# A causal-attention and gated-MLP kernel: fp32r weighted sums issued in one piece, residuals planned behind both copies, and a third matrix group in the weighted sums' bank

## The chip, the cores and the metric

The kernel runs on one core of a Trainium2 chip. The metric is device time in microseconds (us) of one execution, and the median of several. TensorE multiplies 128x128 weights with a stream of columns and adds into banks of PSUM. VectorE (DVE), ScalarE (ACT) and GpSimd (POOL) copy and compute, SyncE (SP) issues the transfers. Each engine works through its own instructions in order and waits on semaphores for the others.

## The reference

```python
scores = scale * np.matmul(q, k.transpose(0, 1, 3, 2))      # q, k, v: (4, 12, 448, 64)
scores = np.where(mask, -1000000000.0, scores)              # causal
attn = np.exp(scores - max); attn = attn / (sum + 1e-09)
attn_out = np.matmul(attn, v)
x = attn_out.transpose(0, 2, 1, 3).reshape(1792, 768)
g = x @ w_gate                                              # (768, 1536)
return ((g / (1 + exp(-g))) * (x @ w_val)) @ w_out          # w_out: (1536, 768)
```

## The kernel before

A chunk is one batch: 448 tokens. There are four, and each has attention for six pairs of heads and then the MLP. The MLP takes 24 matrix groups M0 to M23 of 18 products (gate and value in turn, one bank each) and six output tiles MO0 to MO5 of 36. Every product is a 128x448 fp32r matmul; each tile of weights is used three times (high by high, high by low, low by high part) for the precision, so a chunk has 648 products and the kernel 2592. In what follows a "product" is one of these matmuls (lines 850 to 852).

Attention of chunk 0 runs with plain fp32 matmuls. From chunk 1 on, each pair of heads has: fp32r scores (24 matmuls, line 501), softmax on DVE, ACT and POOL, transposes of the probabilities into a bank T (line 680; line 650 for T_0, which both heads share), a copy of T to `ph` (ACT or DVE, lines 309, 312), a residual T minus `ph` to `pl` or to the other half of `ph` (DVE, line 331), and the weighted sum of the values into the bank O (lines 715 and 717). The weighted sum of a head has seven matmuls: 448 columns for block 0, then twice 384, twice 256 and twice 128. After it ACT copies one half of O to `tmp` and DVE adds the other half into `xs`, which frees O.

PSUM has one bank T (chunk 0 also uses the X banks for transposes), one bank O, two banks M for the matrix groups and two each for S and X. A matrix group needs a bank M for itself until DVE has taken its result out (line 886 for a gate, 892 for a value).

The order of everything is made ahead of the run by `Planner.run`. Each operation `op` has a due time, dependencies, buffers (`Res`) and a modelled length for each engine that can do it; the planner always places the operation that can begin first, the earlier due first, and what it makes is the fixed order of every engine. `TURN` adds time for a change between kinds of TensorE work ("m" product or weighted sum, "s" scores, "t" transposes, "v" fp32 sums), `LAT` is the delay from one engine to another. In `weigh`, each of a head's blocks is an operation of its own with a loop variable `last`; in `spread`, the residual `lo` depends only on its own copy `hi`.

Of the kernel before, what the change touches and what calls it, by code (L numbers as in the profile page):

```python
# [17 lines left out]
P = 128  # L18
D = 64
# [19 lines left out]
SHARED = 0.5  # L39
PVLATE = 0  # L40
LAT = {"PE": 0.29, "DVE": 0.2, "ACT": 0.23, "POOL": 0.2, "SP": 0.1}
TURN = {'ms': 0.19, 'sm': 0.19, 'mt': 0.0, 'tm': 0.0, 'ts': 0.19, 'st': 0.19, 'mv': 0.15, 'vm': 0.15, 'tv': 0.15, 'vt': 0.15, 'sv': 0.15, 'vs': 0.15}
TS = 0.0
PF = 1.12
GF = 1.25
# [1 line left out]
SG = [[[0, 3]], [[1, 2]]]  # L47
TV = 0.0
WINDOW = 96
WARM = 22  # L50
FIRST = [[[0, 1]], [[2]], [[3]]]
KBUS = 1 / 320
# [169 lines left out]
def raw(t):  # L222
    return t.bitcast(F32)
# [3 lines left out]
def kernel(  # L227
# [68 lines left out]
    def op(alts, due, deps=(), alloc=(), uses=(), extra=0.0):  # L296
        first = [heads[r.tag] for r in alloc if r.tag in heads]
        o = pl_.op(alts, due, list(deps) + first, alloc, uses, extra)
        o.soft = first
        o.port = bool(alts.pop("port", False))  # L300
        o.kb = alts.pop("kb", 0)
        o.kind = alts.pop("kind", "m")
        for r in alloc:
            heads[r.tag] = o
        return o
# [83 lines left out]
    def attention(u):  # L389
        U = units[u]  # L390
        c, b, h, N, KB = U.c, U.b, U.h, U.n, U.qb
        s = st[u]
# [220 lines left out]
        def spread(g, js, tr, rT, lo_row, kn, n, cols, offs, v2):  # L613

            stk = kn == D
            rh = Res(f"ph{g}")
            src = lambda: s[f"T{g}"][lo_row : lo_row + kn, :n]

            def newh():
                s[f"ph{g}"] = buf([P, n], F32R, f"ph{g}", "ph", f"ph{u}_{g}")  # L620
                return s[f"ph{g}"][lo_row : lo_row + kn]
            hi = op(copies("psum", n, newh, src, engines="AD"), due(8), [tr], [rh], [rT])
            rl = None if stk else Res(f"pl{g}")

            def newl():
                if stk:
                    return s[f"ph{g}"][D - lo_row : P - lo_row]
                s[f"pl{g}"] = buf([P, n], F32R, f"pl{g}", "pl", f"pl{u}_{g}")
                return s[f"pl{g}"][:kn]
            lo = op(binary(n, newl, src, lambda: raw(s[f"ph{g}"])[lo_row : lo_row + kn], engines="D"),  # L630
                    due(9), [hi], [] if stk else [rl], [rT, rh])
            for j, o_, w in zip(js, offs, cols):
                blocks[j] = (g, o_, w, slice(0, P), stk, [hi, lo, v2], [rh, rV] + ([] if stk else [rl]))

        if h % 2:

            rT = Res(ttag(c))
            both_ = [norms[i] for i in norms] + [normed[u - 1][i] for i in normed[u - 1]]

            def transp0(rT=rT):  # L640
                pt = s["T0"] = st[u - 1]["T0"] = bank(rT.tag, f"T{u}_0")
                for i, (q0, _) in U.qi:
                    r = U.rows[i]
                    w = U.qi[i][1][1]
                    if U.joint and i == 0:

                        o = pt.rearrange("p (a b) -> p a b", b=D)[:, :: N // D]
                        nc.tensor.transpose(o, s["pp0"], ident)
                        continue
                    nc.tensor.transpose(pt[:, q0 : q0 + r], s[f"pp{i}"][:r, w - D : w + D], ident[:r, :r])  # L650
            tr = op({"PE": (0.109 * len(U.qi), transp0), "kind": "t"}, due(7), both_, [rT], list(rps.values()) + ([prps[u - 1][0]] if U.joint else []))
            if npv:
                rh = Res("ph0")

                def newp():
                    s["ph0"] = st[u - 1]["ph0"] = buf([P, NJ], F32, "ph0", "ph", f"ph{u}_0")
                    return s["ph0"]
                NJ = N + D * U.joint
                hi = op(copies("psum", NJ, newp, lambda: s["T0"][:, :NJ], engines="AD"), due(8), [tr], [rh], [rT])
                for y in (0, 1):  # L660
                    parts[u - 1 + y][0] = (0, 0, N, slice(D * y, D * y + D), True, [hi, lv], [rh, rv])
            else:
                first0[u - 1](tr, rT)
                spread(0, [0], tr, rT, D, D, N, [N], [0], v2)
        elif not npv:
            first0[u] = lambda tr, rT: spread(0, [0], tr, rT, 0, D, N, [N], [0], v2)

        for g, js in enumerate([[1], [2, 3]], 1):
            cols = [U.qb - U.base(j) for j in js]
            offs = [sum(cols[:i]) for i in range(len(js))]  # L670
            n = sum(cols)
            rT = Res(ttag(c))
            todo = [(j, o_, i, e) for j, o_ in zip(js, offs) for i, e in U.qi if e[0] >= U.kb[j][0]]

            def transp(g=g, todo=todo, rT=rT):
                pt = s[f"T{g}"] = bank(rT.tag, f"T{u}_{g}")
                for j, o_, i, (q0, q1_) in todo:
                    r, bs, (k0, k1) = U.rows[i], U.base(j), U.kb[j]
                    k0 = k0 if h % 2 else q1_ - k1
                    nc.tensor.transpose(pt[:, o_ + q0 - bs : o_ + q0 - bs + r], s[f"p{i}"][:r, k0 : k0 + P], ident[:r, :r])  # L680
            tr = op({"PE": (0.109 * len(todo), transp), "kind": "t"}, due(7),
                    [norms[i] for i in {i for _, _, i, _ in todo}], [rT], [rps[i] for i in {i for _, _, i, _ in todo}])
            if npv:
                rh = Res(f"ph{g}")

                def newh(g=g, n=n):
                    s[f"ph{g}"] = buf([P, n], F32, f"ph{g}", "ph", f"ph{u}_{g}")
                    return s[f"ph{g}"]
                hi = op(copies("psum", n, newh, lambda g=g, n=n: s[f"T{g}"][:, :n], engines="AD"), due(8), [tr], [rh], [rT])
                for j, o_, w in zip(js, offs, cols):  # L690
                    blocks[j] = (g, o_, w, slice(0, P), False, [hi, lv], [rh, rv])
            else:
                spread(g, js, tr, rT, 0, P, n, cols, offs, v2)
        if h % 2 and not npv:
            weigh(u - 1)
        if h % 2:
# [2 lines left out]
    def weigh(u):  # L699
# [4 lines left out]
        k = h // 2  # L704
        prevx = [xlast[k]] if k in xlast else []
        if not npv:
            rO, last = Res("O"), None
            for j in range(nj):
                g, o_, w, _, stk, dps, use = blocks[j]

                def pv(g=g, j=j, o_=o_, w=w, stk=stk):
                    if j == 0:
                        s["O"] = bank("O", f"O{u}")
                    O, V = s["O"][:, U.base(j) - U.qa : N], s["VS"][:, j, :]
                    nc.tensor.matmul(O, V, s[f"ph{g}"][:, o_ : o_ + w], start=(j == 0), stop=stk and j == nj - 1)  # L715
                    if not stk:
                        nc.tensor.matmul(O, V, s[f"pl{g}"][:, o_ : o_ + w], start=False, stop=(j == nj - 1))  # L717
                last = op({"PE": ((1 if stk else 2) * cost("PE", "r", w), pv)}, due(10), dps + [last],
                          [rO] if j == 0 else [], use + ([rO] if j else []))
            rx, rt = Res(f"xs{h}"), Res("tmp")  # L720

            def newt():
                s["tmp"] = buf([D, S], F32, "tmp", "tmp", f"tmp{u}")[:, :N]
                return s["tmp"]
            t1 = op(copies("psum", N, newt, lambda: s["O"][D:P, :N], engines="AD"), due(11), [last], [rt], [rO])
            o = op(binary(N, lambda: xs[k][D * (h % 2) : D * (h % 2) + D, :N], lambda: s["O"][0:D, :N],
                          lambda: s["tmp"], ALU.add, engines="D"), due(12), [t1] + prevx, [rx], [rO, rt])
            xs_ops.setdefault((c, k), []).append(o)
            xs_res.setdefault((c, k), []).append(rx)
            return  # L730
# [123 lines left out]
    def moe(c):  # L854
# [6 lines left out]
        for f in range(NF):  # L861
            rt = Res("t")
            tops = {}
            for w in range(2):
                gi = 2 * f + w
                i = base + gi
                wh_, wl_, rwh, rwl = wops[i]
                rM = Res("M")
                prev = None
                for k in range(KD):  # L870
                    xa, xb, rxh, rxl = xsplit[c, k]

                    def mm(k=k, f=f, w=w, i=i, gi=gi):
                        if k == 0:
                            ps[c, f, w] = bank("M", f"M{c}_{gi}")
                        mm3(ps[c, f, w], i, k, N, xh[k][:, :N], xl[k][:, :N], k == 0, k == KD - 1)
                    prev = op({"PE": (m3, mm)}, at(gi + k / KD), [prev, wh_, wl_, xa, xb],
                              [rM] if k == 0 else [], [rwh, rwl, rxh, rxl] + ([rM] if k else []))
# [50 lines left out]
    for c in range(NCHUNK):  # L929
# [2 lines left out]
                attention(u)  # L932
        for k in range(KD):
            split_x(c, k)
    for c in range(NCHUNK):
        moe(c)
    order = pl_.run(CAPS)
    with tc.manual_schedule():
# [53 lines left out]
```

## Time and profile before

| what | value |
|---|---|
| median of 3 runs | 697.47 us (696.21 to 697.72) |
| the profiled execution: its time | 697.56 us |
| the profiled execution: its span, first to last instruction | 695.8 us |
| TensorE busy | 685.6 us, 99% of the span |
| DVE, ACT, POOL busy | 353.4, 335.8, 197.1 us |
| granted TensorE clock | 0.999 of full speed |

The span is what the trace shows; 1.8 us of the execution lie around it. The order of TensorE decides the time wherever it is busy, and the other engines matter where TensorE waits for them.

### The profile page before, as it was taken

Reading aid. Unit: us, or ns where it says so; the run is one execution under the profiler, and the core shown is the slowest. Engines: PE = TensorE matmul, PEld = TensorE weight load, DVE = VectorE, ACT = ScalarE, POOL = GpSimd, SP = SyncE. Lnnn points to the kernel's source line nnn. Section 1 sums busy time; section 2 is a strip of 40 time slices with the busy share of each in tenths; the row PEclk is TensorE's granted clock in tenths of the full one; section 3 lists DMA queues with packets and bytes.
Section 4 is the critical chain, followed back from the end, with each engine's and each line's share of the span. In section 5 each row is a group of like instructions: output and inputs, shape, how many; then the busy total and the mean of one; then the engine's idle time right before and its main releaser. Section 6 shows DMA issues by size and latency. Waiting matters only on the chain.

```text
span 695.8 us, 10844 instructions
## 1 busy us (share of the span) xinstructions
PE 685.6 (99%) x3898; PEld 603.3 (87%) x3898; DVE 353.4 (51%) x880; ACT 335.8 (48%) x835; POOL 197.1 (28%) x250
## 2 busy tenths in 40 slices
PE   8998999999999999999999999999999999999998
PEld 6567898898898988888989889999899999999997
DVE  5878977788875453565542255545544222222100
ACT  6997787688583452543543436445455211111000
POOL 3764446366333332332331213223221000000000
PEclk9999999999999999999999999999999999999999
DMA  8778998998988755655657665554466666666671
GB/s 293 267 274 312 374 330 326 338 354 324 355 333 314 253 183 192 209 167 207 203 196 238 214 202 191 183 182 168 151 200 191 193 221 221 199 216 222 213 239 41
DMA packets 40118, 165.08 MB, mean 237 GB/s; under 512 B 4480, under 2 KB 13952, under 8 KB 40064
## 3 DMA queue, kind: packets, MB, share of 16 engines
q1 hardware_dynamic: 39904, 164.28, 68.6%
q8 instruction: 31, 0.51, 0.3%
q14 instruction: 23, 0.19, 0.1%
q10 hardware_dynamic: 160, 0.10, 0.1%
HBM read 130.55 MB, written 33.82 MB: 236 GB/s over the span
## 4 chain that ended last, share of the span: by engine, by line
PE 84%; DVE 3%; ACT 2%; issue 1%; ACTq 0%; DVEq 0%
PE M L850 15%; PE M L851 15%; PE M L852 15%; PE MO L850 9%; PE MO L851 8%; PE MO L852 8%; PE S L501 4%; PE T L680 3%; PE O L715 3%; PE O L717 2%; PE T L650 1%; DVE ph L331 1%; DVE wraw L833 1%; ACT ph L309 1%; ACT top L309 0%
## 5 line engine op out<-in xcount | busy, mean ns | idle before, releaser
L850 PE MATMUL M<-xh,whl 128*128 128x448 f32 x576 | 216.2, 375 | 1.5 <-DVE t L886 1.5
L851 PE MATMUL M<-xl,whl 128*128 128x448 f32 x576 | 210.3, 365 | 0.4 <-DVE xl L331 0.4
L852 PE MATMUL M<-xh,whl 128*128 128x448 f32 x576 | 209.8, 364 | 0.0
L850 PEld LDWEIGHTS M<-xh,whl 128*128 128x128 f32 x576 | 108.1, 188 | 13.3 <-issue 3.5
L852 PEld LDWEIGHTS M<-xh,whl 128*128 128x128 f32 x576 | 107.9, 187 | 9.1
L851 PEld LDWEIGHTS M<-xl,whl 128*128 128x128 f32 x576 | 108.2, 188 | 8.5 <-DVE xl L331 0.8
L850 PE MATMUL MO<-hh,whl 128*128 128x448 f32 x288 | 107.7, 374 | 0.0
L851 PE MATMUL MO<-hl,whl 128*128 128x448 f32 x288 | 105.1, 365 | 0.0
L852 PE MATMUL MO<-hh,whl 128*128 128x448 f32 x288 | 105.0, 364 | 0.0
L551 ACT ACTIVATE p<-p,m 128x192 f32<-128x192 f32 (+3 forms) x180 | 91.0, 508 | 1.8 <-DVE m L540 1.8
L309 ACT ACTIVATE ph<-T 128x384 fp32r<-128x384 f32 (+3 forms) x104 | 51.9, 507 | 65.4 <-PE T L650 35.5
L540 DVE CUSTOM_DVE_ANT_0 p<-S,masks 128x192 f32<-128x192 f32 (+3 forms) x180 | 67.6, 432 | 25.7 <-PE S L501 25.6
L886 DVE SCALAR_TENSOR_TENSOR t<-t,M 128x448 f32<-128x448 f32 x48 | 29.7, 620 | 60.3 <-ACT t L882 60.1
L309 ACT ACTIVATE hh<-t 128x448 fp32r<-128x448 f32 x39 | 22.5, 576 | 76.4 <-DVE t L892 76.2
L599 POOL TENSOR_SCALAR p<-p,rec 128x192 f32<-128x192 f32 (+3 forms) x66 | 39.9, 613 | 64.5 <-DVE rec L563 45.5
L850 PEld LDWEIGHTS MO<-hh,whl 128*128 128x128 f32 x288 | 54.1, 188 | 4.5 <-issue 0.6
L852 PEld LDWEIGHTS MO<-hh,whl 128*128 128x128 f32 x288 | 54.0, 187 | 4.6
L851 PEld LDWEIGHTS MO<-hl,whl 128*128 128x128 f32 x288 | 54.1, 188 | 3.9
L595 ACT ACTIVATE p<-p,rec 128x192 f32<-128x192 f32 (+3 forms) x114 | 49.9, 488 | 10.7 <-DVE rec L563 10.4
L892 DVE TENSOR_TENSOR t<-t,M 128x448 f32<-128x448 f32 x48 | 29.6, 617 | 48.5 <-PE M L852 48.5
L882 ACT ACTIVATE t<-M 128x448 f32<-128x448 f32 x48 | 26.0, 542 | 57.9 <-PE M L852 57.2
L331 DVE TENSOR_TENSOR pl<-T,ph 128x384 fp32r<-128x384 f32 x72 | 39.7, 551 | 25.6 <-ACT ph L309 25.2
(77 smaller groups left out, 864.4 us busy)
## 6 DMA issues: line engine op xcount, KB each, us to landing
whl<-ws SPq DMA_DIRECT2D x108, 768.0 KB, 4.3
wide<-in_w_dram SPq DMA_DIRECT2D x36, 768.0 KB, 6.9
ws<-whl SPq DMA_DIRECT2D x36, 768.0 KB, 6.7
vraw<-in_v_dram SPq DMA_DIRECT2D x24, 256.0 KB, 4.2
out_dram<-osb SPq DMA_DIRECT2D x24, 224.0 KB, 4.7
qraw<-in_q_dram SPq DMA_DIRECT2D x23, 224.0 KB, 4.2
kraw<-in_k_dram SPq DMA_DIRECT2D x23, 224.0 KB, 4.6
qraw<-in_q_dram SPq DMA_DIRECT2D x1, 128.0 KB, 2.4
```

Of the source, the lines that this page charges most:

```text
L309: nc.scalar.activation(out(), in_(), AF.Copy, scale=scale)
L331: r["DVE"] = (cost("DVE", "two", n), lambda: nc.vector.tensor_tensor(out(), a(), b(), alu))
L501: nc.tensor.matmul(st[u + y][f"S{i}"][: U.rows[i]], Q[:, q0 : q0 + U.rows[i]], K[:, :q1_] if y else K[:, S - q1_ :], start=z == 0, stop=z ...
L540: nc.vector.tensor_tensor_reduce(p[:r], s[f"S{i}"][:r], mask[:r, maskX - q0 : maskX - q0 + q1_] if h % 2 else back[:r, P - min(q1_, P) : P ...
L551: nc.scalar.activation(p[:r], p[:r], AF.Exp, bias=peak(i)[:r], scale=-1.0, accum_out=sums[u % NR][:r, i : i + 1],)
L595: nc.scalar.activation(p[:r], p[:r], AF.Copy, scale=rec[u % NR][:r, i : i + 1])
L599: nc.gpsimd.tensor_scalar(p[:r], p[:r], rec[u % NR][:r, i : i + 1], 0.0, ALU.mult, ALU.add)
L850: nc.tensor.matmul(out[:, :n], a[:, w], xhi, start=first, stop=False)
L851: nc.tensor.matmul(out[:, :n], a[:, w], xlo, start=False, stop=False)
L852: nc.tensor.matmul(out[:, :n], l[:, w], xhi, start=False, stop=last)
L886: nc.vector.scalar_tensor_tensor(t, t, 1.0, ps[c, f, 0][:, :N], ALU.add, ALU.mult)
L892: nc.vector.tensor_tensor(t, t, ps[c, f, 1][:, :N], ALU.mult)
```

## The change

Four edits, all of them to what the planner works with.

- A head's weighted sum becomes one operation of kind "o": its seven matmuls stand together, behind all copies and residuals of that head. `TURN` gets four entries for this kind.
- `spread` returns the copy and a function `rest`. For T_0, which two heads share, both copies are made first, and the even head's residual is planned with a dependency on the odd head's copy as well.
- In chunk 0, matrix group M2 (`SPARE`) takes the bank O in place of a bank M.
- `moe(c)` is called right behind the splitting of `x` of its chunk and no more after all attention, which changes ties between equal due times and the order in which users of a bank are numbered.

```diff
-TURN = {'ms': 0.19, ... 'vs': 0.15}
+TURN = {'ms': 0.19, ... 'vs': 0.15, 'om': 0.055, 'os': 0.1, 'so': 0.19, 'ot': 0.03}
+SPARE = [2]
...
-            lo = op(binary(n, newl, src, lambda: raw(s[f"ph{g}"])[lo_row : lo_row + kn], engines="D"),
-                    due(9), [hi], [] if stk else [rl], [rT, rh])
...
+            def rest(first=()):
+                lo = op(binary(n, newl, src, lambda: raw(s[f"ph{g}"])[lo_row : lo_row + kn], engines="D"),
+                        due(9), [hi, *first], [] if stk else [rl], [rT, rh])
...
-                first0[u - 1](tr, rT)
-                spread(0, [0], tr, rT, D, D, N, [N], [0], v2)
+                (_, even), (hi, odd) = first0[u - 1](tr, rT), spread(0, [0], tr, rT, D, D, N, [N], [0], v2)
+                even([hi])
+                odd()
...
-                last = op({"PE": ((1 if stk else 2) * cost("PE", "r", w), pv)}, due(10), dps + [last],
-                          [rO] if j == 0 else [], use + ([rO] if j else []))
+            last = op({"PE": (dur, pv), "kind": "o"}, due(10), dps, [rO], use)
...
-                rM = Res("M")
+                tag = "O" if c == 0 and gi in SPARE else "M"
+                rM = Res(tag)
...
-    for c in range(NCHUNK):
         moe(c)
```

**Place 1, TensorE, the first products of chunk 0.** `M0_g` is matrix group g of chunk 0, `xh5` and `xl5` the last of the six parts of x. Before:

```order
L850 MATMUL M0_0_746<-xh5_82,whl0_452 128x448 [waits Pool_49]
L851 MATMUL M0_0_746<-xl5_88,whl0_452 128x448 [waits DVE_49]
L852 MATMUL M0_0_746<-xh5_82,whl0_452 128x448
L850 MATMUL M0_1_790<-xh5_82,whl1_607 128x448
L851 MATMUL M0_1_790<-xl5_88,whl1_607 128x448
L852 MATMUL M0_1_790<-xh5_82,whl1_607 128x448
L850 MATMUL M0_2_992<-xh0_77,whl2_773 128x448 [waits DVE_49]
```

Now:

```order
L858 MATMUL M0_2_958<-xh0_77,whl2_773 128x448 [waits Activation_49]
L859 MATMUL M0_2_958<-xl0_83,whl2_773 128x448
L860 MATMUL M0_2_958<-xh0_77,whl2_773 128x448
L858 MATMUL M0_0_746<-xh5_82,whl0_452 128x448 [waits Pool_49]
L859 MATMUL M0_0_746<-xl5_88,whl0_452 128x448 [waits DVE_49]
L860 MATMUL M0_0_746<-xh5_82,whl0_452 128x448
L858 MATMUL M0_1_790<-xh5_82,whl1_607 128x448
L859 MATMUL M0_1_790<-xl5_88,whl1_607 128x448
L860 MATMUL M0_1_790<-xh5_82,whl1_607 128x448
L858 MATMUL M0_2_958<-xh1_78,whl2_773 128x448
```

The first three products of group 2 moved ahead of the last ones of groups 0 and 1, and its first product waits for ACT (who emptied bank O) and no more for DVE (who empties a bank M).

**Place 2, TensorE, the weighted sum of the odd head of the last pair** (head 47, bank `O47`; `MO2_5` is the last output tile of chunk 2, and `ph47_0` to `ph47_2` are the copies of the three transposes). Before, in three pieces, with transposes and nine products between:

```order
L715 MATMUL O47_6174<-ph47_0_6133,VS47_5899 128x448 [waits DVE_49]
L680 MATMUL T47_2_6176<-ident_66,p46_2_5991 128x128 [waits DVE_49,PE_49]
L680 MATMUL T47_2_6176<-ident_66,p46_3_5994 128x128 x2
L715 MATMUL O47_6174<-ph47_1_6163,VS47_5899 128x384
L717 MATMUL O47_6174<-pl47_1_6172,VS47_5899 128x384
...
L852 MATMUL MO2_5_6136<-hh6_95,whl107_6044 128x448
L715 MATMUL O47_6174<-ph47_2_6182,VS47_5899 128x256 [waits Activation_49]
L717 MATMUL O47_6174<-pl47_2_6187,VS47_5899 128x256 [waits DVE_49]
L715 MATMUL O47_6174<-ph47_2_6182,VS47_5899 128x128
L717 MATMUL O47_6174<-pl47_2_6187,VS47_5899 128x128
L850 MATMUL MO2_5_6136<-hh7_96,whl107_6044 128x448
```

Now:

```order
L858 MATMUL MO2_5_6135<-hh7_96,whl107_6046 128x448
L859 MATMUL MO2_5_6135<-hl7_108,whl107_6046 128x448
L860 MATMUL MO2_5_6135<-hh7_96,whl107_6046 128x448
L724 MATMUL O47_6196<-ph47_0_6133,VS47_5902 128x448 [waits Activation_49]
L724 MATMUL O47_6196<-ph47_1_6166,VS47_5902 128x384 [waits Activation_49]
L726 MATMUL O47_6196<-pl47_1_6172,VS47_5902 128x384
L724 MATMUL O47_6196<-ph47_2_6184,VS47_5902 128x256 [waits Activation_49]
L726 MATMUL O47_6196<-pl47_2_6191,VS47_5902 128x256 [waits DVE_49]
L724 MATMUL O47_6196<-ph47_2_6184,VS47_5902 128x128
L726 MATMUL O47_6196<-pl47_2_6191,VS47_5902 128x128
L858 MATMUL MO2_5_6135<-hh8_97,whl107_6046 128x448
```

All seven matmuls stand together, in front of the products of `MO2_5`, and no other piece follows. The even head's seven stood together before as well; three more products now stand between T_0 and them at most pairs.

**Place 3, DVE, the last pair of heads**, from the even head's last residuals. Before:

```order
L331 TENSOR_TENSOR ph46_0_6128<-T47_0_6120,ph46_0_6128 64x448 [waits PE_49,Activation_49]
L331 TENSOR_TENSOR ph47_0_6133<-T47_0_6120,ph47_0_6133 64x448
L312 TENSOR_SCALAR ph47_1_6163<-T47_1_6154 128x384 [waits PE_49]
L331 TENSOR_TENSOR xs5_76<-O46_6145,tmp46_6158 64x448 [waits Activation_49]
L331 TENSOR_TENSOR pl47_1_6172<-T47_1_6154,ph47_1_6163 128x384 [waits DVE_49]
L331 TENSOR_TENSOR pl47_2_6187<-T47_2_6176,ph47_2_6182 128x384 [waits Activation_49]
L331 TENSOR_TENSOR xs5_76<-O47_6174,tmp47_6204 64x448 [waits Activation_49]
```

Now:

```order
L332 TENSOR_TENSOR ph46_0_6128<-T47_0_6120,ph46_0_6128 64x448 [waits PE_49,Activation_49]
L332 TENSOR_TENSOR ph47_0_6133<-T47_0_6120,ph47_0_6133 64x448
L332 TENSOR_TENSOR xs5_76<-O46_6149,tmp46_6161 64x448 [waits Activation_49]
L332 TENSOR_TENSOR pl47_1_6172<-T47_1_6157,ph47_1_6166 128x384 [waits Activation_49]
L332 TENSOR_TENSOR pl47_2_6191<-T47_2_6177,ph47_2_6184 128x384 [waits Activation_49]
L332 TENSOR_TENSOR xs5_76<-O47_6196,tmp47_6207 64x448 [waits Activation_49]
```

The two residuals of T_0 (`ph46_0`, `ph47_0`) stand one behind the other in both programs. The copy of T_1 went from DVE to ACT, so the add into `xs` now comes directly before the residual of T_1.

## Rows read from the trace of the kernel before

**Rows 1.** The page's first part: busy us, share of span, instructions by engine.

```profile
PE 685.6 (99%) x3898; PEld 603.3 (87%) x3898; DVE 353.4 (51%) x880; ACT 335.8 (48%) x835; POOL 197.1 (28%) x250
```

**Rows 2.** The list of waits: us in total, times, longest.

```profile
PEld O L715 <- DVE ph L331: 5.9, 15, 0.7
PE M L850 <- DVE t L886: 1.5, 1, 1.5
```

**Rows 3.** Timeline, TensorE, 58.6 to 63 us: start, length, line, tiles, count [wait].

```profile
58.90 0.36 PE L850 MATMUL M<-xh,whl 128*128 128x448 f32 x1
...
59.64 0.47 PE L851 MATMUL M<-xl,whl 128*128 128x448 f32 x1 [0.39 <-DVE xl L331]
...
60.56 0.36 PE L852 MATMUL M<-xh,whl 128*128 128x448 f32 x1
...
62.38 0.47 PE L850 MATMUL M<-xh,whl 128*128 128x448 f32 x1 [1.47 <-DVE t L886]
```

**Rows 4.** Timeline, DVE, 61 to 63 us.

```profile
61.72 0.61 DVE L886 SCALAR_TENSOR_TENSOR t<-t,M 128x448 f32<-128x448 f32 x1
```

**Rows 5.** Timeline, TensorE, 374 to 378 us: T_0, products, a weighted sum, T_1.

```profile
374.42 0.60 PE L650 MATMUL T<-ident,p 128*128 128x128 f32 x4
...
376.51 0.36 PE L852 MATMUL MO<-hh,whl 128*128 128x448 f32 x1
...
376.85 0.65 PE L715 MATMUL O<-ph,VS 128*128 128x448 f32 x2
...
377.34 0.34 PE L717 MATMUL O<-pl,VS 128*128 128x384 f32 x1
...
377.94 0.52 PE L680 MATMUL T<-ident,p 128*128 128x128 f32 x3
```

**Rows 6.** Timeline, ACT and then DVE, 375 to 379 us.

```profile
375.06 1.09 ACT L309 ACTIVATE ph<-T 64x448 fp32r<-64x448 f32 x2 [2.29 <-PE T L650]
...
378.14 0.54 ACT L309 ACTIVATE tmp<-O 64x448 f32<-64x448 f32 x1 [1.99 <-PE O L717]
...
376.18 1.27 DVE L331 TENSOR_TENSOR ph<-T,ph 64x448 fp32r<-64x448 f32 x2 [5.89 <-ACT ph L309]
...
379.08 0.62 DVE L331 TENSOR_TENSOR xs<-O,tmp 64x448 f32<-64x448 f32 x1
```

**Rows 7.** Timeline, TensorE, 159.5 to 161.3 us: a weighted sum's first three matmuls.

```profile
159.94 0.54 PE L715 MATMUL O<-ph,VS 128*128 128x448 f32 x2
160.32 0.34 PE L717 MATMUL O<-pl,VS 128*128 128x384 f32 x1
```

**Rows 8.** Timeline, TensorE, 133 us: products behind a whole weighted sum.

```profile
132.99 0.42 PE L850 MATMUL M<-xh,whl 128*128 128x448 f32 x1
133.24 0.37 PE L851 MATMUL M<-xl,whl 128*128 128x448 f32 x1
133.45 0.37 PE L852 MATMUL M<-xh,whl 128*128 128x448 f32 x1
```

**Rows 9.** Timeline, TensorE, 367 to 368 us: products, two others between these.

```profile
367.48 0.36 PE L850 MATMUL MO<-hh,whl 128*128 128x448 f32 x1
...
368.08 0.36 PE L850 MATMUL MO<-hh,whl 128*128 128x448 f32 x1
```

**Rows 10.** Timeline, TensorE, from 555 us: behind the last weighted sum, and the last product.

```profile
555.14 0.42 PE L850 MATMUL MO<-hh,whl 128*128 128x448 f32 x1
555.40 0.36 PE L851 MATMUL MO<-hl,whl 128*128 128x448 f32 x1
555.60 0.36 PE L852 MATMUL MO<-hh,whl 128*128 128x448 f32 x1
555.81 0.37 PE L850 MATMUL MO<-hh,whl 128*128 128x448 f32 x1
...
692.00 0.36 PE L852 MATMUL MO<-hh,whl 128*128 128x448 f32 x1
```

More of the change, by code (lines that the diff above doesn't have):

```diff
@@ L41 @@
 LAT = {"PE": 0.29, "DVE": 0.2, "ACT": 0.23, "POOL": 0.2, "SP": 0.1}
-TURN = {'ms': 0.19, 'sm': 0.19, 'mt': 0.0, 'tm': 0.0, 'ts': 0.19, 'st': 0.19, 'mv': 0.15, 'vm': 0.15, 'tv': 0.15, 'vt': 0.15, 'sv': 0.15, 'vs': 0.15}
+TURN = {'ms': 0.19, 'sm': 0.19, 'mt': 0.0, 'tm': 0.0, 'ts': 0.19, 'st': 0.19, 'mv': 0.15, 'vm': 0.15, 'tv': 0.15, 'vt': 0.15, 'sv': 0.15, 'vs': 0.15, 'om': 0.055, 'os': 0.1, 'so': 0.19, 'ot': 0.03}
 TS = 0.0
@@ L629, in newl @@
                 return s[f"pl{g}"][:kn]
-            lo = op(binary(n, newl, src, lambda: raw(s[f"ph{g}"])[lo_row : lo_row + kn], engines="D"),
-                    due(9), [hi], [] if stk else [rl], [rT, rh])
-            for j, o_, w in zip(js, offs, cols):
-                blocks[j] = (g, o_, w, slice(0, P), stk, [hi, lo, v2], [rh, rV] + ([] if stk else [rl]))
+            def rest(first=()):
+                lo = op(binary(n, newl, src, lambda: raw(s[f"ph{g}"])[lo_row : lo_row + kn], engines="D"),
+                        due(9), [hi, *first], [] if stk else [rl], [rT, rh])
+                for j, o_, w in zip(js, offs, cols):
+                    blocks[j] = (g, o_, w, slice(0, P), stk, [hi, lo, v2], [rh, rV] + ([] if stk else [rl]))
+            return hi, rest
         if h % 2:
@@ L692, in attention @@
             else:
-                spread(g, js, tr, rT, 0, P, n, cols, offs, v2)
+                spread(g, js, tr, rT, 0, P, n, cols, offs, v2)[1]()
         if h % 2 and not npv:
@@ L706, in weigh, with pv @@
         if not npv:
[L707 to L713, printed above, removed]
+            rO, dps, use, dur = Res("O"), [], [], 0.0
+            for g, o_, w, _, stk, d_, r_ in (blocks[j] for j in range(nj)):
+                dps += [x for x in d_ if x not in dps]
+                use += [r for r in r_ if r not in use]
+                dur += (1 if stk else 2) * cost("PE", "r", w)
+            def pv():
+                s["O"] = bank("O", f"O{u}")
+                for j in range(nj):
+                    g, o_, w, _, stk, _, _ = blocks[j]
                     O, V = s["O"][:, U.base(j) - U.qa : N], s["VS"][:, j, :]
@@ L871, in moe, with mm @@
                     xa, xb, rxh, rxl = xsplit[c, k]
-                    def mm(k=k, f=f, w=w, i=i, gi=gi):
+                    def mm(k=k, f=f, w=w, i=i, gi=gi, tag=tag):
                         if k == 0:
-                            ps[c, f, w] = bank("M", f"M{c}_{gi}")
+                            ps[c, f, w] = bank(tag, f"M{c}_{gi}")
                         mm3(ps[c, f, w], i, k, N, xh[k][:, :N], xl[k][:, :N], k == 0, k == KD - 1)
```

## The prediction

> **What bounds the kernel now.** I read the page's first part first: TensorE is busy 685.6 of 695.8 us [rows 1], so the time is the sum of what TensorE does, one thing behind the other, and an edit pays only where TensorE's row of starts gets closer. Then the list of waits, and there the entries of TensorE and of its weight loads alone: 5.9 us in 15 waits of a weighted sum's first weight load for DVE's residual, and one of 1.5 us for DVE's gate product [rows 2]. DVE's or ACT's own idle time says nothing here. Then the timeline of TensorE, read by starts, since lengths overlap: what counts is the distance from one start to the next. Three things are to be seen.
>
> First, chunk 0 stalls once. The second product of group 0's last part starts 0.74 us after the first (59.64 against 58.90), and group 2's first product starts 1.82 us after the one ahead of it (62.38 against 60.56) [rows 3]. An undisturbed distance is 0.20 us [rows 9]. The second stall ends when DVE has finished the gate product that began at 61.72 and took 0.61 [rows 4]: group 2 waits for the bank of group 0.
>
> Second, the even head's weighted sum waits at most pairs. The last product ahead starts at 376.51, the sum at 376.85: 0.34 where 0.20 is usual, so 0.14 is lost. The first two matmuls of the sum then take 0.49 (377.34 less 376.85) [rows 5], where a sum that came late enough takes 0.38 [rows 7]: another 0.11. A wait costs 0.25 us. What it waits for [rows 6]: ACT copies T_0 for both heads from 375.06 to 376.15, and only then, at 376.18, DVE starts the two residuals, the first of which ends near 376.81. I count 14 such waits in TensorE's starts from 186.7 to 548.7, two of them longer (0.18 and 0.25 instead of 0.14).
>
> Third, the products have two spacings. Three products take 0.60 us [rows 9], 200 ns each. Behind the last weighted sum they take (692.00 - 555.81) / 659 = 206.7 ns each, to the end [rows 10]. The clock is granted in full all along. A stretch keeps the spacing with which it began until transposes or scores interrupt it. By starts, 1008 of the distances between products are slow ones, 659 in the last stretch. The difference, 6.7 ns, is 4.4 us there and 2.3 us in the 349 others. How a stretch begins shows which it will be: a second distance of 201 to 203 ns leads to 206.7, one of 204 (twice 200) leads to 200. Behind twelve pieces of four matmuls (two of 256 columns, two of 128) the second distance is 0.20 (555.60 less 555.40) and the stretch slow; the last of them is in [rows 10]. Behind a whole sum of seven it is 0.21 (133.45 less 133.24) in the one place that has it, 133 us [rows 8], too short to show the stretch itself.
>
> **The change part by part**, against the profiled 697.56 us (0.09 above the median of 697.47).
>
> *Third group in bank O.* Of the two stalls, 1.62 + 0.54 us beyond the usual 0.20, and 0.1 behind each at the next distance (59.64 to 59.95 is 0.31 instead of 0.20), make 2.37. Group 2 no longer waits for group 0's bank, and its first three products (0.60) stand ahead of the product that waited 0.54. Group 3, which needs the bank now, comes 18 products later, about 63.7, when the gate product (ended 62.33) is done. I take 2.0 and not 2.37: chunk 0 keeps DVE and ACT busiest, and some of the lead will be met there by later transposes. Bounds: 0 (all met later) to 2.4. Bank O is free by then (fp32 sums of chunk 0 are over) and needed again only for the first fp32r sum, some 15 us on.
>
> *The residuals.* The two stand on DVE as before, one behind the other and behind both copies; so nothing on DVE or ACT gets quicker. What moves is TensorE's order: three more products stand between T_0 and the even sum, twelve where there were nine, 0.6 us. The sum then comes near 377.3 by [rows 5] (0.14 late before, so 0.46 early now). The twelve usual waits give 3.0 and the two long ones 0.64: 3.6 us. Bounds: 0 if DVE is late by another 0.5, 4.2 if the wait near 77 us (0.5 and 0.1) goes too.
> The Trainium skill ("TensorE: Matmul & The Clock Gate", section "Architectural detail: the array is 16× 32×32, not 1× 128×128") says that TensorE can pull weight loads ahead of running matmuls. By that rule the weights of the sum's second matmul would be in place when the wait ends, the 0.11 would not be the wait's, and this item would be 2.1 us. The trace speaks against it: 0.49 beside 0.38.
>
> *One piece.* The odd head's sum stood in three parts: first matmul, transposes, two matmuls, nine products, four matmuls. Each join costs some hundredths: by starts, three parts with their transposes take 1.38 us beyond the products, and one whole sum (0.96 and 0.06 at its end) with transposes alone (0.34) takes 1.36. That is 0.02 for each of 18 pairs, 0.3 us; bounds 0 to 0.6.
>
> *Spacing.* What precedes the last 660 products is no longer the four matmuls but the whole seven, entered from fast products (transposes stand nine products ahead, and behind three transposes stretches run fast). This is the state of [rows 8], whose sign is the fast one. If it holds, 660 x 6.7 ns = 4.4 us, and the others go from 349 slow distances to some 230, 0.8 us less (about 130 in the twelve products behind each T_0, which stay slow, and half of the 170 behind sums that follow scores). Bounds: 0.4 worse (all the stretches behind sums slow too) to 6.0 better. The semaphore waits on the sum's inner matmuls are the doubt; products that carry a met wait for a weight tile keep their distance.
>
> *New waits.* The trace of before has 2.9 us of scattered waits besides those named. The order is dealt anew, and I take as many again plus 1.0, mostly for T_2 (below). Bounds 0 to 3.
>
> Sum: 2.0 + 3.6 + 0.3 + 4.4 + 0.8 - 1.0 = 10.1; 697.56 - 10.1 = **687.5 us**, with a range of its own from 684.8 to 690.
>
> **The rivals.** *The last stretch stays slow.* The sum ends with the same four matmuls as the pieces that led to slow spacing twelve times of twelve. Then the 4.4 and the 0.8 fall away, and 0.4 is lost: 697.56 - 4.9 + 0.4 = 693.1, give or take 1.5. For it: twelve cases; against: one case, but of the very same kind.
>
> *The gains come back as waits in chunk 0 and behind the residuals.* The lead of 2.0 is spent on transposes waiting for ACT's and DVE's softmax, and DVE is late again at T_0: little remains, 694 to 697. For it: DVE and ACT are busiest in chunk 0; against: the later waits there are few.
>
> *T_2 waits at every pair (slower).* T_2 needs bank T back, that is T_1's residual. That residual now stands on DVE behind the add into `xs`, which waits for ACT's `tmp`, and the copy of T_1 stands on ACT behind `tmp`. By [rows 6] `tmp` ends at 378.68, the copy takes 0.49 to 379.17, the add ends at 379.34, the residual (0.56) at 379.90. T_1 began at 377.94 [rows 5], and nine products lead to T_2 near 380.10: 0.2 to spare. If DVE has one more operation of 0.62 in between, T_2 waits 0.4 at that pair and loses another 0.1 behind it. At all 18 pairs that is 9 us, and with the last stretch slow the kernel ends near 701. It decides from 0.3 us a pair. In the new order only two or three pairs have such an operation, so the chance is small.
>
> *The change moves nothing:* excluded; the orders differ from place 1 on.
>
> **How the numbers follow.** Forecast 0.5, last stretch slow 0.32, gains come back 0.12, T_2 waits 0.06. The range from 684.8 to 694.2 takes in nearly all of the first and four fifths of the second and a little of the third, 0.8 in all. A difference of 0.2% (1.4 us) is about what a measurement of this kernel can tell from none. Below 696.1 lie the first two cases and two thirds of the third: faster 0.90; the rest of the third 0.05 the same; slower 0.05.
>
> **What would show it.** In the profile after: no wait of group 2 for DVE's gate product; 0.20 us and not 0.34 ahead of the even sums, and 0.38 for their first two matmuls; the last 660 products in 132.0 us (fast) or 136.4 (slow), which alone decides between the first two cases; TensorE's waits for T in sum below 4 us. I would be wrong if DVE's residuals are late again, if weight tiles come too late in chunk 0 now that TensorE leads, or if spacing follows something that I have not seen.

## The result, and the profile after

The changed kernel takes 687.91 us (median of 4 runs, 687.77 to 688.73) beside 697.59 for the kernel before: ratio 0.9868, 95% interval 0.9851 to 0.9885. Forecast were 687.5 us, range 684.8 to 694.2. The profiled execution took 687.97 us with a span of 686.2. These views of its profile answer to those of before. First the page's busy line and the list of waits (us in total, times, longest):

```profile
PE 675.1 (98%) x3898; PEld 604.4 (88%) x3898; DVE 353.9 (52%) x866; ACT 347.5 (51%) x864; POOL 193.9 (28%) x235
```

```profile
PE T L686 <- DVE pl L332: 2.8, 4, 1.4
...
PEld O L724 <- DVE ph L332: 1.6, 2, 1.2
...
PE O L724 <- DVE ph L332: 0.8, 1, 0.8
PE MO L860 <- DVE whl L332: 0.5, 1, 0.5
```

TensorE is still the bound. The wait for DVE's gate product [rows 2] is gone, that of the sums' weight loads (PEld) for their residual has shrunk from 5.9 us in 15 cases to 1.6 us in two, and a new one leads the list: transposes for the bank T. The timeline of TensorE (start, length, line, tiles, count, wait) shows, in this order: chunk 0 where group 2 stalled before [rows 3], the new wait, an even sum [rows 5], and the last stretch [rows 10].

```profile
58.45 0.36 PE L858 MATMUL M<-xh,whl 128*128 128x448 f32 x1
58.65 0.42 PE L859 MATMUL M<-xl,whl 128*128 128x448 f32 x1
58.91 0.37 PE L860 MATMUL M<-xh,whl 128*128 128x448 f32 x1
59.11 0.36 PE L858 MATMUL M<-xh,whl 128*128 128x448 f32 x1
...
66.45 0.36 PE L860 MATMUL M<-xh,whl 128*128 128x448 f32 x1
68.20 0.52 PE L686 MATMUL T<-ident,p 128*128 128x128 f32 x3 [1.39 <-DVE pl L332]
...
373.56 0.37 PE L860 MATMUL MO<-hh,whl 128*128 128x448 f32 x1
373.77 0.54 PE L724 MATMUL O<-ph,VS 128*128 128x448 f32 x2
374.15 0.34 PE L726 MATMUL O<-pl,VS 128*128 128x384 f32 x1
...
550.54 0.42 PE L858 MATMUL MO<-hh,whl 128*128 128x448 f32 x1
550.80 0.37 PE L859 MATMUL MO<-hl,whl 128*128 128x448 f32 x1
551.00 0.36 PE L860 MATMUL MO<-hh,whl 128*128 128x448 f32 x1
551.21 0.36 PE L858 MATMUL MO<-hh,whl 128*128 128x448 f32 x1
...
682.40 0.36 PE L860 MATMUL MO<-hh,whl 128*128 128x448 f32 x1
```

Chunk 0 runs through, with 0.05 us left of the two stalls. The transposes at 68.20 come 1.75 us behind the product ahead, 1.55 too late. The even sum follows 0.21 us after the last product, and its first two matmuls take 0.38. The last 660 products take (682.40 - 550.54) / 659 = 200.1 ns each.

The first product of chunk 0 starts at 41.87 us before and at 40.85 after, although nothing that the change touches lies ahead of it; in the twelve profiles of this study it starts between 39.8 and 42.1. So kernels are compared below by the time **from the first product's start to the last one's** as well: 650.13 us before, 641.55 after, 8.6 us less.

### The profile page after: what moved, and what is told of

Read it like the earlier page. It is cut to its first block, busy times and chain, and to the rows that moved or that the text cites. A ratio compares the mean times of both kernels' runs of the same rounds, so it can differ in the third digit from the quotient of the medians.

```text
span 686.2 us, 10835 instructions
## 1 busy us (share of the span) xinstructions
PE 675.1 (98%) x3898; PEld 604.4 (88%) x3898; DVE 353.9 (52%) x866; ACT 347.5 (51%) x864; POOL 193.9 (28%) x235
## 4 chain that ended last, share of the span: by engine, by line
PE 85%; ACT 8%; DVE 5%; issue 1%; DMA 0%; POOL 0%; ACTq 0%
PE M L858 15%; PE M L859 15%; PE M L860 15%; PE MO L858 8%; PE MO L859 7%; PE MO L860 7%; PE S L502 5%; PE T L686 4%; PE O L724 3%; ACT p L552 3%; ACT p L596 2%; PE O L726 2%; PE T L654 1%; ACT top L310 1%; DVE p L541 1%
## 5 line engine op out<-in xcount | busy, mean ns | idle before, releaser
L310 ACT ACTIVATE ph<-T 128x384 fp32r<-128x384 f32 (+3 forms) x116 | 57.7, 504 | 57.0 <-PE T L654 34.7
L596 ACT ACTIVATE p<-p,rec 128x192 f32<-128x192 f32 (+3 forms) x130 | 58.8, 503 | 8.9 <-DVE rec L564 8.5
L686 PE MATMUL T<-ident,p 128*128 128x128 f32 x288 | 47.2, 277 | 3.2 <-DVE pl L332 2.8
```

The source lines that it names most:

```text
L310: nc.scalar.activation(out(), in_(), AF.Copy, scale=scale)
L596: nc.scalar.activation(p[:r], p[:r], AF.Copy, scale=rec[u % NR][:r, i : i + 1])
```

## The experiments

The table has the runs whose times are compared. A kernel made by an edit to the planner's input ("no third bank", "residuals as before", "sums in pieces" and "the same, no third bank") has the orders of all engines dealt anew, so it can differ from its partner in more places than the edit names; in the runs that only leave out the addition or add pieces to TensorE, the rest of each engine's order stays. The two runs with 26 pieces (one execution each, 702.20 and 700.18 us) served for their traces alone.

| kernel | median us | ratio to before, 95% interval | first to last product, us |
|---|---|---|---|
| before (beside these) | 696.0 to 696.7 | | 650.13 |
| changed, again | 687.79 | 0.9872 (0.9855 to 0.9889) | 641.67 |
| no third bank | 688.5 | 0.9884 (0.9866 to 0.9901) | 641.79 |
| residuals as before | 690.07 | 0.9911 (0.9898 to 0.9924) | 644.21 |
| sums in pieces | 693.83 | 0.9964 (0.9951 to 0.9978) | 648.03 |
| before, three transposes more | 692.5 | 0.9939 (0.9927 to 0.9952) | 647.10 |
| changed, no addition | 682.74 | 0.98 (0.9784 to 0.9816) | 636.52 |
| the same, no third bank | 683.14 | 0.9809 (0.9791 to 0.9826) | 636.91 |
| before, no addition | 693.42 | 0.9965 (0.9952 to 0.9979) | 649.06 |

**Each part of the change undone by itself.** First the third bank:

```diff
-SPARE = [2]
+SPARE = []
```

> The changed kernel with group 2 of chunk 0 back in a bank M; all else as changed. Theory: the two stalls of chunk 0 come back (group 2 waits near 60 us for DVE's gate product, 2.4 us with the distances behind them), but the new wait of 1.5 us for bank T near 66 us goes, since it stands there only because TensorE leads; so the edit was worth about 0.8 us and this kernel takes about 688.7 us. Rival: the two are not connected, the wait near 66 us stays, and it takes about 690.2 us.

```profile
59.25 0.36 PE L860 MATMUL M<-xh,whl 128*128 128x448 f32 x1
61.07 0.47 PE L858 MATMUL M<-xh,whl 128*128 128x448 f32 x1 [1.46 <-DVE t L895]
```

The two stalls are back (59.25 to 61.07 where 0.20 is usual, waiting for DVE's gate product), 2.4 us with the distances behind them; the wait near 66 us is gone. But the kernel is only 0.1 to 0.2 us longer than the changed one from first to last product. The theory held in its direction, but even less of the gain is left than the 0.8 us that it named.

Then the residuals:

```diff
-                (_, even), (hi, odd) = first0[u - 1](tr, rT), spread(0, [0], tr, rT, D, D, N, [N], [0], v2)
-                even([hi])
-                odd()
+                first0[u - 1](tr, rT)[1]()
+                spread(0, [0], tr, rT, D, D, N, [N], [0], v2)[1]()
```

> The changed kernel with the residuals planned as before (the even head's right behind its own copy); nine products instead of twelve stand between T_0 and the even sum again at most pairs. Theory: the even sum's wait for its residual comes back at some 12 pairs, 0.14 us ahead of it and 0.11 at its second matmul each, so 3.0 to 3.6 us: about 691.2 us, with the last stretch still at 200.0 ns. Rival: the sum in one piece alone took these waits away and the residual edit is worth nothing: about 688 us.

Fourteen even sums wait again, 2.2 us ahead of them. Timeline of TensorE in this kernel, at the pair of [rows 5]:

```profile
374.83 0.36 PE L859 MATMUL MO<-hh,whl 128*128 128x448 f32 x1
375.18 0.64 PE L723 MATMUL O<-ph,VS 128*128 128x448 f32 x2
375.66 0.34 PE L725 MATMUL O<-pl,VS 128*128 128x384 f32 x1
```

0.35 ahead of the sum instead of 0.21, and 0.48 for its first two matmuls instead of 0.38: both halves of the quarter of a microsecond are the wait's. The kernel is 2.6 us longer; the last stretch stays at 200.0 ns. The rival (one piece alone takes the waits away) falls.

Then the pieces, with the old loop over blocks in `weigh`:

```diff
-            last = op({"PE": (dur, pv), "kind": "o"}, due(10), dps, [rO], use)
+                last = op({"PE": ((1 if stk else 2) * cost("PE", "r", w), pv)}, due(10), dps + [last],
+                          [rO] if j == 0 else [], use + ([rO] if j else []))
```

> The changed kernel with each block of a weighted sum an operation of its own as before; the last stretch of 660 products then follows four matmuls instead of seven. Theory: those 660 run at 206.7 ns (4.4 us), the stretches behind the other such pieces too (about 0.8), and the joins cost 0.3: about 693.4 us. Rival: the spacing comes from when the stretch begins and not from the piece ahead of it; then the last stretch stays at 200.0 ns and the time is about 688.3 us.

```profile
553.79 0.27 PE L723 MATMUL O<-pl,VS 128*128 128x128 f32 x1
553.90 0.42 PE L856 MATMUL MO<-hh,whl 128*128 128x448 f32 x1
554.15 0.36 PE L857 MATMUL MO<-hl,whl 128*128 128x448 f32 x1
554.36 0.36 PE L858 MATMUL MO<-hh,whl 128*128 128x448 f32 x1
...
690.13 0.36 PE L858 MATMUL MO<-hh,whl 128*128 128x448 f32 x1
```

In this timeline the last stretch takes (690.13 - 553.90) / 659 = 206.7 ns each again, 4.4 us more. By starts there are 1127 slow distances; the changed kernel has 206, the kernel before 1008. All eleven stretches of seven products or more behind four matmuls that follow products directly are slow. The kernel is 6.4 us longer, the dearest of the three undone parts; the 921 slow distances more are 6.2 us of it.

**The spacing, changed alone.** Into the kernel before, three products behind the last sum:

```diff
+    SLOTS = ['t3']
...
+            if r == 0 and 0 <= i < len(SLOTS):
+                extra(SLOTS[i], wi)
```

> The kernel before with one addition: three transposes of the identity into the free bank T, three products behind the last weighted sum; what they write is read by nobody. Theory: how a stretch of products is spaced is set by what stands right ahead of it; behind three transposes the last 660 run at 200.0 ns instead of 206.7, 4.4 us less, and the transposes cost 0.35 to 0.45: about 693.6 us. Rival: the spacing goes with this order of the program as a whole, and the three transposes only add their 0.4: about 698.0 us.

```profile
555.24 0.49 PE L854 MATMUL extra<-ident 128*128 128x128 f32 x3
555.48 0.45 PE L867 MATMUL MO<-hh,whl 128*128 128x448 f32 x1
555.77 0.37 PE L868 MATMUL MO<-hl,whl 128*128 128x448 f32 x1
...
687.38 0.36 PE L869 MATMUL MO<-hh,whl 128*128 128x448 f32 x1
```

The 660 products behind them take 200.1 ns each, and 4.0 us of 696.46 are gone for 0.33 us of useless work (in the profile, and so in the table's last column, it is only 3.0: some 1.5 us went to the clock near 62 us, as in the last section). So a short piece ahead of the stretch can change its spacing, in a program whose order is otherwise the same, and the rival falls. Whether the form of that piece decides was asked next, in the changed kernel:

```diff
+    SLOTS = ['t4', 't3', 't4', 't1', 't4', 't2', 't4', 't5', 't4', 't6', 't4', 't7', 't4', 'o4', ...]
```

> The changed kernel with 26 short pieces put into its last stretch of 660 products, one every 24 products, all into the free bank T and read by nobody: one to seven transposes of the identity (t1 to t7), and fp32r matmuls of a weight tile with 128 columns (o1), with 448, 384, 384 (o3), 256, 256, 128, 128 (o4) and the seven of a weighted sum (o7). Mostly a t4 stands between two others, so that each form is entered from slow products. Theory: the piece right ahead of a stretch of products sets its spacing, whatever the spacing was before: behind t4 and o4 some 206.7 ns, behind t3 and o7 200.0 ns. Rival: a piece only flips or keeps the spacing that was there; then t3 entered from slow and from fast products would differ. A third: an odd number of matmuls gives fast and an even number slow; then t1, t5 and t7 would give 200.0, t2 and t6 206.7.

Behind four transposes the stretch was slow five times of ten, behind the four matmuls never (two). One, five and seven transposes gave slow, fast, fast, two and six fast and slow; three (four times), `o7`, `o1` (twice each) and `o3` fast. So neither the form nor an odd or even number decides, and my theory falls as it was put. The first rival was not tested by the three transposes, since all four were entered from fast products. Two places in the timeline of this kernel, with the same four transposes:

```profile
577.35 0.60 PE L862 MATMUL extra<-ident 128*128 128x128 f32 x4
577.70 0.45 PE L875 MATMUL M<-xh,whl 128*128 128x448 f32 x1
577.99 0.36 PE L876 MATMUL M<-xl,whl 128*128 128x448 f32 x1
578.20 0.36 PE L877 MATMUL M<-xh,whl 128*128 128x448 f32 x1
...
587.76 0.60 PE L862 MATMUL extra<-ident 128*128 128x128 f32 x4
588.12 0.45 PE L875 MATMUL M<-xh,whl 128*128 128x448 f32 x1
588.40 0.37 PE L876 MATMUL M<-xl,whl 128*128 128x448 f32 x1
588.61 0.36 PE L877 MATMUL M<-xh,whl 128*128 128x448 f32 x1
```

The first stretch is slow, the second fast. They begin alike but for 3 ns: the first two distances are 290 and 201 ns by the trace's nanoseconds in the slow one, 287 and 204 in the fast one.

A second run, with repeated pieces:

```diff
+    SLOTS = ['t4'] * 9 + ['o4'] * 9 + ['t1'] * 4 + ['t6'] * 4
```

> The changed kernel with 26 pieces in its last stretch, one every 24 products, into the free bank T: nine times four transposes, nine times four matmuls (256, 256, 128, 128 columns), four times one transpose, four times six transposes. In the first such look four transposes led to slow spacing five times of eleven, the four matmuls never of two. Theory: the piece's form does not decide; the spacing follows the phase in which the first products behind it start, so four transposes give both spacings again, and a second distance of 204 or more goes with 200.0 ns and one of 203 or less with 206.7 in every case. Rival: the form does decide, and what was ahead in the first look was the difference: then each form gives one spacing only, from its second time on.

(Where this expectation says five of eleven, it was five of ten.) Four transposes: three slow, six fast, in the order fast, fast, slow three times over. One transpose: one slow, three fast; six: four fast; the four matmuls: nine fast. So the rival falls: one form gives both spacings. In all 52 pieces of the two runs a second distance of 204 ns or more led to 200.0, one of 203 or less to 206.7. That is a sign of the spacing and not its cause; that it follows a phase, as the theory says, is not shown, though the regular order of the nine fits.

**What holds DVE up.** The new wait at 68.20 ends with DVE's residual `pl`. Timelines of DVE and of GpSimd in the changed kernel:

```profile
65.78 1.62 DVE L563 TENSOR_SCALAR rec<-sums 128x4 f32<-128x4 f32 x1 [0.18 <-ACT p L552]
67.44 0.18 DVE L564 RECIPROCAL rec<-rec 128x4 f32<-128x4 f32 x1
67.53 0.53 DVE L332 TENSOR_TENSOR pl<-T,ph 128x384 fp32r<-128x384 f32 x1
```

```profile
65.55 1.82 POOL L335 TENSOR_TENSOR whl<-wraw,whl 128x768 fp32r<-128x768 f32 x1
```

An addition of 1e-9 to four row sums in each of 128 partitions takes 1.62 us and ends at 67.40; GpSimd's instruction, begun 0.23 us before it, ends at 67.37. The view of that line says that this is no usual length (shortest, median, longest in ns):

```profile
L563 DVE TENSOR_SCALAR rec<-sums x48: 154/170/1622, 9.4 to 531.0; 128x4 f32<-128x4 f32 x42, 128x3 f32<-128x3 f32 x6
```

The waits for T at 398 and 505 us stand behind two more of the long ones (1.12 and 0.68 us). In this profile 14 of the 48 additions take over 0.25 us, 8.4 us beyond the median in sum, and every one of them ends 0.02 to 0.03 us behind a GpSimd instruction that began before it; in the kernel before they are nine, 5.2 us beyond.
The Trainium skill ("SBUF — State Buffer", section "Who interferes with whom") says that VectorE and GpSimd share a pair of ports, that `tensor_scalar` can take it in its two-port modes, and that who comes second is blocked until the other's instruction ends. The trace agrees at this place: 67.40 beside 67.37. The planner models such a lock, but this operation is not marked for it.

```diff
-            nc.vector.tensor_scalar(rc, sm, 1.0e-9, None, ALU.add)
-            nc.vector.reciprocal(rc, rc)
+            nc.vector.reciprocal(rc, sm)
```

> The changed kernel without the addition of 1e-9 to the row sums ahead of the reciprocal (a sum holds at least exp(0) = 1, and 1 + 1e-9 is 1 in fp32, so the values are the same); the order of every engine stays as in the changed kernel, 48 DVE instructions of 0.16 us fall out. Theory: three of the waits for T that are left (1.55 us at 66.5, 0.79 at 398, 0.34 at 505) are DVE's, because this addition, 0.16 us long elsewhere, takes 1.62, 1.12 and 0.68 us there, and ends each time when a GpSimd instruction ends that began before it; without it the residual behind it comes in time, 2.7 us less: about 685.2 us, first to last product 638.9 us instead of 641.6. Rival: DVE is late there for other reasons, or the reciprocal now waits in the same way: within 0.5 us of the changed kernel.

```profile
64.69 0.18 DVE L564 RECIPROCAL rec<-sums 128x4 f32<-128x4 f32 x1 [0.18 <-ACT p L552]
64.79 0.53 DVE L332 TENSOR_TENSOR pl<-T,ph 128x384 fp32r<-128x384 f32 x1
```

```profile
64.18 1.85 POOL L335 TENSOR_TENSOR whl<-wraw,whl 128x768 fp32r<-128x768 f32 x1
```

The reciprocal takes its 0.18 us in the middle of the same GpSimd instruction (64.18 to 66.03), the residual follows at once, and TensorE's waits for T at 66, 398 and 505 us are gone. None of the 48 reciprocals takes over 0.18 us, and 21 of them begin inside a GpSimd instruction. The gain is larger than expected: 5.1 us. TensorE's stalls from 30 us on, by starts, fall from 6.9 to 2.4 us: besides the three waits (2.7), smaller ones of chunk 0's sums and of T behind other additions. Spacing takes another 0.2 (173 slow distances instead of 206). At 682.74 us this version beats both kernels.

The changed kernel itself, beside it:

> The changed kernel as it is, beside the others on the same chip. Both theories: the time between first and last product as in its first profile, 641.6 us within 0.3, with the waits of 1.55, 0.79 and 0.34 us for bank T at the same places; what lies ahead of the first product may differ by a microsecond, as it did between the profiles so far (40.3 to 42.1 us).

It did so: 641.67 us, the waits 1.38, 0.80 and 0.35, the first product at 40.09.

Then both edits, to see whether the third bank's lead lasts now:

```diff
-SPARE = [2]
+SPARE = []
...
-            nc.vector.tensor_scalar(rc, sm, 1.0e-9, None, ALU.add)
```

> The kernel without the addition, and with group 2 of chunk 0 back in a bank M. Theory: the third bank gained only 0.2 us, first to last product, because the 2.4 us that it saves near 60 us were spent on the wait of 1.55 us near 66 us and on others behind it; with the addition gone the lead lasts, and this kernel is 1.5 to 2.4 us slower than the one without the addition and with the third bank. Rival: the lead meets DVE's or ACT's backlog of chunk 1 all the same; then the two are within 0.6 us.

The theory falls: without the addition too the third bank is worth only 0.4 us. The lead of 2.4 is spent elsewhere: with the bank, TensorE waits 0.97 us at 101.7 for an even sum's residual, 0.27 at 200.2 for a weight tile and 0.46 at 213.6 for T; without it these are gone and one of 0.26 stands at 90.4. That leaves 0.9; spacing takes 0.2 of it (173 slow distances beside 143), and some 0.3 I can't place. The wait at 101.7 is DVE's once more. In the kernel without the addition and with the third bank, TensorE, DVE and GpSimd there, and the view of DVE's line 841 (shortest, median, longest in ns):

```profile
102.89 0.65 PE L724 MATMUL O<-ph,VS 128*128 128x448 f32 x2 [0.81 <-DVE ph L332]
```

```profile
100.46 1.73 DVE L841 SCALAR_TENSOR_TENSOR wraw<-wide,top 128x768 uint32<-128x768 uint32 x1 [0.47 <-ACT top L310]
```

```profile
99.52 1.85 POOL L335 TENSOR_TENSOR whl<-wraw,whl 128x768 fp32r<-128x768 f32 x1 [4.10 <-ACT whl L310]
```

```profile
L841 DVE SCALAR_TENSOR_TENSOR wraw<-wide,top x36: 922/959/1917, 16.8 to 208.0; 128x768 uint32<-128x768 uint32 x36
```

The residual that the sum needs stands behind an instruction of 1.73 us whose median is 0.96 and which began beside one of GpSimd. No run takes this overlap away, so its price is not shown.

Last, the same two DVE lines changed in the kernel before:

> The kernel before without the addition of 1e-9 to the row sums (the values are the same); the order of every engine stays as before, 48 DVE instructions fall out. In the changed kernel this was worth 5.0 us. Theory: the addition's waits for GpSimd cost the kernel before less, since TensorE comes later there and waits at fewer of those places (0.80 us at 402, 0.29 at 269, and about 0.5 ahead of 58 us): 1.5 to 3 us less, about 694.4 us beside 696.7. Rival: they are as dear in both kernels, and the new wait at 66 us is not the change's doing: 5 us less, about 691.7 us.

2.4 us less by the ratio, so the addition cost the kernel before half as much as the changed one. The lead from the third bank is not the reason: without that bank the addition costs as much, 641.79 less 636.91 or 4.9 us, with other waits in place of the one at 68.20. The new orders hold more additions up (14 and 13 places with and without the bank, nine before); what else makes them dearer stays open. In this profile another 1.5 us went to the clock. Busy time by stretch in this kernel (stretch, its length, busy us and instructions of PE, PEld, DVE, ACT, POOL, the granted clock, the share of DMA, GB/s):

```profile
58.00:60.00 2.00, 0.52 (x3) 0.30 (x2) 2.00 (x10) 2.00 (x8) 1.35 (x2) 1.00 0.99 402
60.00:62.00 2.00, 2.00 (x7) 1.75 (x7) 1.45 (x6) 1.60 (x6) 1.09 (x2) 0.54 0.99 414
62.00:64.00 2.00, 2.00 (x7) 1.80 (x7) 2.00 (x2) 1.68 (x5) 1.00 (x1) 0.61 0.51 202
64.00:66.00 2.00, 2.00 (x13) 1.83 (x12) 0.68 (x1) 0.94 (x2) 0.00 (x0) 1.00 0.74 296
```

## Why the prediction was right

The steps, by the time between first and last product (predicted 10.1 us less, measured 8.6):

| term | predicted | measured |
|---|---|---|
| third bank: the stalls near 60 us | -2.0 (2.37 of stall) | -2.3 |
| even sums | -3.6 | -2.8 |
| one piece, its joins | -0.3 | -0.3 (the rest) |
| spacing, last stretch and others | -5.2 | -5.3 |
| new waits | +1.0 | +2.1 |

Measured are, by starts in the two profiles: the stalls of chunk 0, 2.37 before and 0.05 after; the waits ahead of and in the even sums, 4.2 before and 1.4 after; 1008 - 206 slow distances at 6.6 ns; and the other waits, 3.0 before and 5.15 after. The 1.0 us by which the first product happened to start earlier lay outside the sum; the forecast comes out 0.4 off because it made up for most of the 1.5 that was missing, and that is luck.

*Spacing.* The largest term was right in sign, place and size: 200.1 ns, 131.9 us for the last 660 products. Counting stretches of seven products or more, in seven profiles all 90 right behind a whole sum are fast; in four all 43 behind four matmuls that follow products are slow; behind T_0, over ten profiles, 159 of 175 are. What the prediction inferred from this, that the form of the piece sets the spacing, is not so: put elsewhere, the same four matmuls gave fast spacing eleven times of eleven. What sets it in the first products stays open. The rival "the last stretch stays slow" lost its 0.32 on the fact that was against it, the one row of the very same kind. Half of the forecast rested on that single case; that it was the rule was seen only afterwards.

*The residuals.* Right as reasoned, shown by undoing them: 2.6 us come back, both halves of the quarter microsecond. The rule on weight loads that the prediction set aside would have given 2.1; its 0.11 at the second matmul came back as well. Mis-sized was what is left: "0 if DVE is late by another 0.5" happened at one pair (0.97 at 104), the wait near 214 stayed (0.21), and the one near 77 us went, which the 3.6 had left out.

*The third bank.* This step failed in its size: "I take 2.0 and not 2.37 ... some of the lead will be met there by later transposes". Nearly all of it was met: undone, it costs 0.1 to 0.2 us. The first transposes to meet it were those at 68.20, 1.55 us late, but the rest went later. Counted where both orders have the same work behind them, the changed kernel is ahead of the one without the bank by 2.4 us after 40 products, 0.8 after 80 (70 us), and 2.7 after 180 (96 us), since the other then waits too, 0.7 us for a sum's residual at 76 and 1.1 for T at 92; it is still 1.7 ahead after 540 (193 us) and 0.1 after 870 (279 us). Between these two lie waits that the other order has not: 0.64 us for a weight tile at 204, 0.21 at 214 and 0.75 for T at 218. So the rival "the gains come back as waits", 0.12, was half right: it came for the lead of chunk 0, up to 218 us, and not for the residuals.

*New waits.* This term was too small: put at 1.0, they were 2.1. Most of them are the same fact: up to some 220 us DVE has little slack, and a lead of TensorE there turns into waits for it. The additions held up by GpSimd stood in the trace of before, and I had looked at what TensorE waits for, not at why DVE is late.

*T_2 at every pair* did not come: four waits of T for a residual, 2.8 us in sum, below the 4 that the prediction named, and three of the four places (68, 398 and 505 us) stand behind a long addition.

## What to carry to other kernels

A stall removed early in a stage where another engine has no slack is a lead that later waits can take back, here within some 160 us; price it by undoing the edit, not by the length of the stall, and look at where the two runs part and meet, since undoing deals the orders anew. Where a wait ends with an engine, look at that engine's instructions for one that is far longer than its median, and at what runs beside it: here an addition on four numbers a partition, which could simply be left out, was worth 5 us. Compare kernels by the starts of the bounding engine's work, since the time ahead of it can move by 2 us from run to run.

## What the runs showed of the hardware

- Products of 128x448 run at two stable distances, 200.0 and 206.7 ns, at a granted clock of 1.00; three useless transposes ahead of 660 of them saved 4.4 us for 0.33. The second distance tells which it will be: 204 ns or more went with the first, 203 or less with the second, 52 times of 52.
- A DVE addition on 128x4 fp32 numbers, 0.17 us by its median, took up to 1.62 us while GpSimd worked; a reciprocal of the same shape was not held up under the same GpSimd instruction. That GpSimd holds it is read from ends that agree, 14 of 14 long ones in the changed kernel and nine of nine in the kernel before, and from the gain of leaving it out.
- In the kernel before without the addition, no product starts between 57.87 and 59.70 us; in the two stretches of 2 us that follow the granted clock is 0.54 and 0.61 (the rows above), with nine products 0.37 us apart, the 1.2 GHz level; in the profile of the kernel before the clock stayed at 1.00 behind the same stall. With the third bank, which takes that stall away, none of 27 executions has a mean granted clock below 0.999; of 48 in kernels that keep the stall, 11 have 0.998 or less. In the kernel without the bank two such took 689.1 and 689.2 us, the two at 1.000 687.9 and 687.2. So in some executions the bank is worth more than its 0.1 to 0.2 us.
